# A gated linear attention feeding a SiLU layer: weights to float32 by bits, products read from PSUM, the reverse scan first, and a range check that reads its data late

## The chip, the cores and the metric

The kernel runs on one core of a Trainium2 chip. The core has five engines with a queue each: PE (TensorE, matrix products), DVE (VectorE), ACT (ScalarE), POOL (GpSimd) and SP (SyncE, which here only issues DMAs). Each works off its queue in order and waits on semaphores for the others. The metric is the device time of one execution in microseconds (us). The kernel before takes 747.67 us (median of 3 runs, 747.03 to 749.17).

## The reference

```python
# q, k, v, alpha: float32 (4, 8, 768, 48); moe_w_in (384, 2048), moe_w_out (2048, 384): float64
state = zeros(B, H, D, D)
for t in range(S):
    state = alpha[:, :, t, :, None] * state + einsum('bhd,bhe->bhde', k[:, :, t], v[:, :, t])
    y[:, :, t] = einsum('bhd,bhde->bhe', q[:, :, t], state)
x = y.transpose(0, 2, 1, 3).reshape(B * S, H * D)          # (3072, 384)
h = x @ w_in
out = (h * (1.0 / (1.0 + exp(-h))) @ w_out).astype(float32)
```

`alpha` lies between 0.8 and 1. Both weight matrices arrive as float64 (two 32-bit words an element, 512 KB for a piece of 128 by 512).

## The kernel before

**Chunks.** The sequence is cut into 6 chunks of 128 tokens for each of 4 batches: 24 chunks, numbered n, four batches after each other for one stretch of the sequence. A chunk passes through four stages. `products`: PE transposes a, k and q of the chunk (L484), ACT copies them out of PSUM (L486, L489), DVE builds the running product `p` of alpha forward (a scan, L493), its end (`least`, L497) and the end's reciprocal (`inv`, L498), and backward products `r` by a second scan (L499) that starts from `inv`; POOL multiplies q by `p` (L501) and DVE k by `r` (L502). `scores`: PE forms k·q for 8 heads (L513), DVE masks them (`g`, L517), PE transposes the scaled k back (L521) and ACT copies it (L523). `values`: PE multiplies the scores by v (L530), adds q times the carried state (L535), ACT copies the result (`x`, L539); PE then forms the chunk's addition to the state (L543), DVE adds it (L548) and POOL multiplies the state by the chunk's decay (L550). `bridge`: PE transposes the result into the layout of the next layer (L560), ACT copies it (`xt`, L561).

**The layer.** `moe` takes one stretch (4 chunks, 512 tokens): 16 pieces of 3 products each (L570) with a SiLU behind each on ACT (L573), then 4 outputs of 16 products each (L579), copied by ACT (L584) and stored (L586). That is 32 pieces a stretch, 192 in all; they are the filler that PE works on between chunk stages.

**Weights.** A piece of float64 is loaded by SP (L453), and turned into float32 by nine instructions: four on DVE (L456, L459, L461, L464), three on POOL (L457, L458, L465), one on ACT (L463). There are 12 pieces of `w_in` and 16 of `w_out`.

**Order.** A loop over 27 steps emits stage `products` of chunk `step`, `scores` of the chunk before it, `values` of the one before that, `bridge` of the one before that; behind each stage it emits weight pieces (steps 0 to 7: `w_in`) or layer pieces up to a share that grows evenly. A layer piece is held back until its four chunks have passed `bridge`. A scheduler behind the language then fixes each engine's queue; it may move an instruction past others of the program. PSUM tiles: `ps_t` (2 buffers), `ps_g`, `ps_y`, `ps_s` (1 each), `ps_m` (2).

**Check.** The largest |alpha| of every chunk (`most`, L477) and the smallest decay are kept; at the end they give a flag. If it is 0, a second, general function runs everything again.

## Time and profile before

| | |
|---|---|
| median of 3 runs | 747.67 us |
| the profiled execution's own time | 747.51 us |
| its span, first to last instruction | 745.8 us |
| PE busy | 690.5 us (93%) |
| DVE, ACT, POOL busy | 226.5, 157.5, 126.4 us |
| mean granted clock of PE | 0.941 |
| moved by DMA | 36.74 MB |

The page gives the busy share of each engine in 40 slices of the span (18.6 us each), and the clock granted to PE in the same slices. PE counts as busy while matmuls are in flight, at whatever clock; so a busy PE at clock 0.5 does half the work. In the lists of the profile a matmul of float32 stands as two records (a transpose as one); "x96" in the chain counts records. A time behind "<-" is idle time that ended when the named engine delivered.

### The profile page before, as it was taken

How to read it: one execution, taken by the hardware profiler on the slowest of the kernel's cores; microseconds unless marked ns; L12 is line 12 of the kernel's file. 1: busy time of each engine (PE TensorE's matmuls, PEld its weight loads, DVE VectorE, ACT ScalarE, POOL GpSimd, SP SyncE). 2: the span in 40 equal slices, each digit the busy share in tenths (PEclk: the TensorE clock that was granted, in tenths of full speed). 3: DMA queues.
4: the chain of work that ended last, by engine and by line, in shares of the span. 5: the costliest groups of instructions: out<-in, count | busy, mean ns of one | idle time of the engine just before them, and what ended most of it. 6: DMA issues, size and time to landing. Idle time of an engine off the chain costs nothing.

```text
span 745.8 us, 7166 instructions
## 1 busy us (share of the span) xinstructions
PE 690.5 (93%) x2874; PEld 428.9 (58%) x2874; DVE 226.5 (30%) x353; ACT 157.5 (21%) x290; POOL 126.4 (17%) x155
## 2 busy tenths in 40 slices
PE   4657779997899999999999999999999999999996
PEld 2656755554565556674556684456674456754553
DVE  4898695447422121212213142002171001000000
ACT  2322223322212221122211122211132210122100
POOL 4467364335311010100101010001010000000000
PEclk9755598998999999999999989999999999999999
DMA  9767377315220102031010221011010000000000
GB/s 155 150 140 158 91 133 136 88 53 137 64 53 22 33 11 43 22 68 28 11 32 25 50 54 22 0 22 32 19 26 1 0 11 11 22 2 1 0 21 25
DMA packets 107371, 36.74 MB, mean 49 GB/s; under 512 B 100672, under 2 KB 103744, under 8 KB 107328
## 3 DMA queue, kind: packets, MB, share of 16 engines
q1 hardware_dynamic: 107328, 36.19, 23.6%
q8 instruction: 25, 0.41, 0.2%
q14 instruction: 18, 0.15, 0.1%
HBM read 31.46 MB, written 4.72 MB: 49 GB/s over the span
## 4 chain that ended last, share of the span: by engine, by line
PE 82%; DVE 10%; POOL 2%; issue 1%; ACT 1%; DMA 1%; SPq 1%; ACTq 0%; POOLq 0%; DVEq 0%
PE ps_m L570 33%; PE ps_m L579 30%; PE ps_y L530 5%; PE ps_g L513 4%; PE ps_t L484 3%; PE ps_y L535 2%; PE ps_s L543 2%; DVE r L499 2%; DVE p L493 2%; PE ps_t L521 1%; DVE g L461 1%; DVE g L464 1%; DVE g L459 1%; POOL st L550 1%; DVE g L456 1%
## 5 line engine op out<-in xcount | busy, mean ns | idle before, releaser
L579 PE MATMUL ps_m<-w_out,g 128*128 128x384 f32 x768 | 257.8, 490 | 6.6 <-POOL w_out L465 6.6
L570 PE MATMUL ps_m<-xt,w_in 128*128 128x512 f32 x576 | 254.4, 597 | 1.3 <-ACT g L573 0.8
L579 PEld LDWEIGHTS ps_m<-w_out,g 128*128 128x128 f32 x768 | 143.3, 191 | 101.6 <-POOL w_out L465 9.5
L570 PEld LDWEIGHTS ps_m<-xt,w_in 128*128 128x128 f32 x576 | 108.4, 192 | 128.0 <-issue 125.9
L573 ACT ACTIVATE g<-ps_m 128x512 f32<-128x512 f32 x96 | 57.2, 597 | 192.2 <-PE ps_m L570 192.2
L550 POOL TENSOR_TENSOR st<-st,p 128x384 f32<-128x384 f32 x20 | 19.1, 955 | 316.9 <-DVE st L548 258.4
L517 DVE TENSOR_TENSOR g<-ps_g,mask 128x512 f32<-128x512 f32 x48 | 31.1, 684 | 135.2 <-PE ps_g L513 135.0
L513 PE MATMUL ps_g<-qt,kt 48*128 48x128 f32 x384 | 36.8, 330 | 27.3 <-DVE kt L502 26.5
L530 PEld LDWEIGHTS ps_y<-vn,g 128*128 128x128 f32 x384 | 51.7, 209 | 11.0 <-issue 7.1
L530 PE MATMUL ps_y<-vn,g 128*128 128x48 f32 x384 | 51.6, 286 | 5.1 <-issue 4.1
L513 PEld LDWEIGHTS ps_g<-qt,kt 48*128 48x128 f32 x384 | 30.7, 226 | 39.8 <-issue 19.9
L501 POOL TENSOR_TENSOR qt<-qt,p 128x512 f32<-128x512 f32 x24 | 29.9, 1246 | 125.5 <-ACT qt L489 91.9
L548 DVE TENSOR_TENSOR st<-ps_s,st 48x192 f32<-48x192 f32 x40 | 14.2, 355 | 102.5 <-PE ps_s L543 102.0
L477 DVE TENSOR_REDUCE most<-an 128x1 f32<-128x512 f32 x24 | 16.2, 679 | 79.0 <-DMA an<-in_alpha_dram 79.0
L499 DVE TENSOR_TENSOR_SCAN r<-al,inv 128x516 f32<-128x516 f32 x24 | 39.3, 1639 | 0.6
L584 ACT COPY o<-ps_m 128x384 f32<-128x384 f32 x24 | 11.5, 479 | 129.9 <-PE ps_m L579 114.8
L493 DVE TENSOR_TENSOR_SCAN p<-al,one 128x516 f32<-128x516 f32 x24 | 30.5, 1270 | 18.6 <-POOL st L550 15.3
L502 DVE TENSOR_TENSOR kt<-kt,r 128x512 f32<-128x512 f32 x24 | 17.7, 737 | 59.5 <-ACT kt L489 57.7
L489 ACT COPY qt<-ps_t 128x512 f32<-128x512 f32 x24 | 14.0, 585 | 61.7 <-PE ps_y L535 56.4
L463 ACT ACTIVATE g<-g 128x384 f32<-128x384 int32 (+1 forms) x28 | 16.0, 570 | 51.0 <-DVE g L461 40.2
L464 DVE SCALAR_TENSOR_TENSOR g<-bits,g 128x384 f32<-128x384 uint32 (+1 forms) x28 | 19.6, 699 | 22.2 <-ACT g L463 22.1
L484 PE MATMUL ps_t<-ident,an 128*128 128x128 f32 x96 | 18.8, 330 | 7.9 <-DMA an<-in_alpha_dram 4.8
(56 smaller groups left out, 430.5 us busy)
## 6 DMA issues: line engine op xcount, KB each, us to landing
bits<-in_moe_w_in_dram SPq DMA_DIRECT2D x12, 512.0 KB, 3.8
bits<-in_moe_w_out_dram SPq DMA_DIRECT2D x16, 384.0 KB, 3.3
an<-in_alpha_dram SPq DMA_DIRECT2D x24, 192.0 KB, 4.1
kn<-in_k_dram SPq DMA_DIRECT2D x24, 192.0 KB, 4.0
qn<-in_q_dram SPq DMA_DIRECT2D x24, 192.0 KB, 4.3
vn<-in_v_dram SPq DMA_DIRECT2D x24, 192.0 KB, 2.9
out_dram<-o SPq DMA_DIRECT2D x24, 192.0 KB, 1.9
```

Source lines behind the costliest of these rows:

```text
L464: dve.scalar_tensor_tensor(m, lo, 2.0**-52, m, ALU.mult, ALU.add)
L484: pe.transpose(ps[:, j, :], c[name][:, 2 * j : 2 * j + 2, :], ident)
L493: dve.tensor_tensor_scan(p[:, 0 : n_all - 1], sg[:, 0 : n_all - 1], one[:, 0 : n_all - 1], 0.0, ALU.mult, ALU.add)
L499: dve.tensor_tensor_scan(r[:, n_all - 2 :: -1], sg[:, n_all - 1 : 0 : -1], iv[:, n_all - 2 :: -1], 0.0, ALU.mult, ALU.add)
L501: gps.tensor_tensor(out["q"], out["q"], tokens(p), ALU.mult)
L513: pe.matmul(ps[:, u, j, :], lhsT=c["kp"][r, j, :], rhs=c["qp"][r, j, :], start=True, stop=True)
L517: dve.tensor_tensor(g[:, u], ps[:, u], mask[:, None, :].to_broadcast([128, NP, C]), ALU.mult)
L530: pe.matmul(py[:, h, :], lhsT=g[:, h % 2, h // 2, :], rhs=vn[:, h, :], start=(h == 0), stop=(ci == 0 and h == H - 1), skip_group_check=True)
L550: gps.tensor_tensor(s, s, c["pc"][:, :, None].to_broadcast([128, NP, 2 * D]), ALU.mult)
L570: pe.matmul(ps, lhsT=w_in[:, t, f * 128 : (f + 1) * 128], rhs=xt[:, t, :], start=(t == 0), stop=(t == NKT - 1))
L573: act.activation(gf, ps, AF.Silu)
L579: pe.matmul(ps, lhsT=gs[f][:, b * C : (b + 1) * C], rhs=w_out[:, f, :], start=(f == 0), stop=(f == NFT - 1))
```

## The change

- **Weights by bits.** A piece takes five instructions and none on POOL: ACT scales the low words into `up`; DVE shifts and masks the high words into the weight tile, ors in the two top bits, and adds `up` as integers. The built program shows that addition as one instruction of its own kind over 16-bit halves (1024 to a row of 512 words).
- **Products.** `u`, the backward products, come first, from a scan that starts from ones; the forward scan `p` then starts from the reciprocal of the chunk's decay (`all`). DVE multiplies k and q straight from PSUM, so two ACT copies and a POOL product a chunk are gone. `ps_t` has 3 buffers in place of 2, and `ps_s` is gone: the state's addition uses `ps_y` too.
- **State.** A function of its own, `states`, emitted behind `bridge`; the decay is multiplied in ahead of it, in `scores`, on DVE.
- **Check.** `most` is gone. `audit` reads alpha again (9 pieces of 512 KB) and both weight matrices again (28 pieces), each reduced by DVE: the largest of alpha, largest and smallest exponent word of the weights. Up to two audit pieces are emitted a step from step 10 on.
- **Schedule.** 5 slots a step; `w_in` in steps 1 to 6, the layer from step 7 (before: 0 to 7, from 8); `w_out` two pieces ahead of each layer piece. `raw`, the buffers of the loads, 4 in place of 2.
- The memsets on POOL ahead of the first scan are in another order.

```diff
-    raw = pool("raw", 2)
+    raw = pool("raw", 4)
-    gpool = pool("gpool", NFT + 4)
+    gpool = pool("gpool", NFT + 3)
-    ps_t = pool("ps_t", 2, PS)
+    ps_t = pool("ps_t", 3, PS)
-    ps_s = pool("ps_s", 1, PS)
...
-    for t in seg + inv:
-        gps.memset(t, 0.0)
+    gps.memset(seg[0], 0.0)
     gps.memset(one, 0.0)
     gps.memset(one[:, 0 : NP * W + 1 : W], 1.0)
+    for t in inv + seg[1:]:
+        gps.memset(t, 0.0)
...
-            e = gpool.tile([128, 512], I32, name="g")[:, 0:n]
-            dve.tensor_scalar(e, hi, 20, 0x7FF, ALU.logical_shift_right, ALU.bitwise_and)
-            gps.tensor_scalar(e, e, 1151, 896, ALU.min, ALU.max)
-            gps.tensor_scalar(e, e, -896.0, float(1 << 23), ALU.add, ALU.mult)
-            dve.scalar_tensor_tensor(e, hi, -(1 << 31), e, ALU.bitwise_and, ALU.bitwise_or)
...
-            gps.tensor_tensor(dst, m, e.bitcast(F32), ALU.mult)
+            up = gpool.tile([128, 512], I32, name="g")[:, 0:n]
+            act.activation(up, lo, AF.Copy, scale=2.0**-29)
+            w = dst.bitcast(I32)
+            dve.tensor_scalar(w, hi, 3, 0x3FFFFFFF, ALU.logical_shift_left, ALU.bitwise_and)
+            dve.scalar_tensor_tensor(w, hi, -(1 << 30), w, ALU.bitwise_and, ALU.bitwise_or)
+            dve.tensor_tensor(w, w, up, ALU.add)
             yield
...
+    def audit():
+        flat = alpha.rearrange("b h s d -> (b h s d)").rearrange("(p c) -> p c", p=128)
+        todo = [(flat[:, c : c + AW], AW, 0) for c in range(0, flat.shape[1], AW)]
+        if wide:
+            todo += [(moe_w_in[t * 128 : t * 128 + 128, c : c + 512], 512, 1)
+                     for c in range(0, DF, 512) for t in range(NKT)]
+            todo += [(moe_w_out[f * 128 : f * 128 + 128, :], HD, 1) for f in range(NFT)]
...
+        for src, n, kind in todo:
+            t = raw.tile([128, 512, 2], I32, name="bits")
...
+            for which, op in ((0, ALU.max), (1, ALU.min)):
+                if kind == 1 or which == 0:
+                    dve.tensor_reduce(seen[kind][which][:, i : i + 1], x, axis=AX, op=op,
+                                      apply_absolute_value=True)
+            yield
...
+        u = work.tile([128, end + 1], F32, name="u")
+        dve.tensor_tensor_scan(u[:, end - 1 :: -1], sg[:, end:0:-1], one[:, end:0:-1],
                                0.0, ALU.mult, ALU.add)
...
-        gps.tensor_tensor(out["q"], out["q"], tokens(p), ALU.mult)
-        dve.tensor_tensor(out["k"], out["k"], tokens(r), ALU.mult)
+        dve.tensor_tensor(kp, ps["k"], tokens(u), ALU.mult)
...
+        dve.tensor_tensor_scan(p[:, 0:end], sg[:, 0:end], iv[:, 0:end], 0.0, ALU.mult, ALU.add)
+        dve.tensor_tensor(qp, ps["q"], tokens(p), ALU.mult)
...
+        if ci > 0:
+            s = st[b].rearrange("p j u e -> p j (u e)")
+            dve.tensor_tensor(s, s, c["all"][:, :, None].to_broadcast([128, NP, 2 * D]), ALU.mult)
...
+    def states(n):
...
+            ps = ps_y.tile([128, NP, 2, D], F32, name="ps_y")
...
+    def fill(step, slot):
+        nonlocal done
+        if step < FIRST:
+            if step >= 1:
+                convert(0, ((step - 1) * SLOTS + slot + 1) * n_conv[0] // ((FIRST - 1) * SLOTS))
+            return
+        if step > FIRST + 2 and slot in (0, 2):
+            next(audits, None)
+        share = total * ((step - FIRST) * SLOTS + slot + 1) // (SLOTS * (STEPS - FIRST))
+        while done < share and done // PIECES * B + B <= bridged:
+            convert(1, 2 * done + 2)
+            next(filler)
+            done += 1
```

The instructions change place in the queues. Three places matter below.

DVE, in the start, chunk 7 before (p to kt: L493 to L502; L456 to L464 belong to weight pieces):

```order
L493 SCALAR_TENSOR_TENSOR p<-al_141,one 128x516
L517 TENSOR_TENSOR g<-ps_g,mask 128x512
L497 TENSOR_SCALAR least<-p 128x4
L517 TENSOR_TENSOR g<-ps_g,mask 128x512
L498 RECIPROCAL inv_143<-least 128x4
L459 SCALAR_TENSOR_TENSOR g<-bits,g 128x512
L499 SCALAR_TENSOR_TENSOR r<-al_141,inv_143 128x516
L461 TENSOR_SCALAR g<-bits 128x512
L502 TENSOR_TENSOR kt<-kt,r 128x512
```

DVE, the same start, now: from the forward scan of chunk 5 to the backward scan of chunk 6 (L522 `u`, L530 `p`, L532 `qp`, L588 the state out of `ps_y`, L464 to L466 two weight pieces):

```order
L530 SCALAR_TENSOR_TENSOR p<-al_138,inv_140 128x516
L464 TENSOR_SCALAR w_in<-bits 128x512
L532 TENSOR_TENSOR qp<-ps_t,p 128x512
L465 SCALAR_TENSOR_TENSOR w_in<-bits,w_in 128x512
L464 TENSOR_SCALAR w_in<-bits 128x512
L466 ISA w_in<-w_in,g 128x1024
L465 SCALAR_TENSOR_TENSOR w_in<-bits,w_in 128x512
L588 COPY st_154<-ps_y 48x4x48
L466 ISA w_in<-w_in,g 128x1024
L588 COPY st_154<-ps_y 48x4x48
L522 SCALAR_TENSOR_TENSOR u<-al_137,one 128x516
```

The state leaves `ps_y` behind six instructions of two weight pieces, and the next chunk's scan stands behind it.

PE, in the start, now: from the scores of chunk 5 to the state of chunk 4 (L543 scores, L551 k back, L598 bridge, L563 and L568 values, L517 the next chunk's a, L608 the layer, L580 the state):

```order
L543 MATMUL ps_g<-qp,kp 128x128 x8
L551 MATMUL ps_t<-ident,kp 128x128 x4
L598 MATMUL ps_t<-ident,x 128x128 x3
L563 MATMUL ps_y<-vn,g 128x48 x8
L568 MATMUL ps_y<-st_151,qp 128x96 x4
L517 MATMUL ps_t<-ident,an_101 128x128 x4
L608 MATMUL ps_m<-xt,w_in 128x512
L580 MATMUL ps_y<-vn,kn 128x96 x4
```

Values (L563) need `ps_y` free, so they wait for the second L588 above; the next chunk's a stands behind them.

DVE, later, now: chunk 9, with the audit's reductions (L499) between its own instructions:

```order
L522 SCALAR_TENSOR_TENSOR u<-al_138,one 128x516
L499 TENSOR_REDUCE seen_1225<-bits 128x1
L525 TENSOR_TENSOR kp<-ps_t,u 128x512
L527 TENSOR_SCALAR least<-u 128x4
L556 TENSOR_TENSOR st_152<-st_152,u 128x384
L528 RECIPROCAL inv_140<-least 128x4
L499 TENSOR_REDUCE seen_1226<-bits 128x1
L530 SCALAR_TENSOR_TENSOR p<-al_138,inv_140 128x516
L499 TENSOR_REDUCE seen_1225<-bits 128x1
L499 TENSOR_REDUCE seen_1226<-bits 128x1
L547 TENSOR_TENSOR g<-ps_g,mask 128x512 x2
```

In the kernel before, a chunk at this place has one reduction of its own (L477) and the last pieces of `w_out`; now the queue of DVE carries all 65 reductions of the audit between the scan of chunk 8 and that of chunk 11, and each waits for its load.

133 lines of the change are left out of this document (67 added, 66 removed).

## The prediction

> **What bounds the kernel now.** First the page: busy shares, the slices, and the chain of waits by engine.
>
> ```profile
> PE 690.5 (93%) x2874; PEld 428.9 (58%) x2874; DVE 226.5 (30%) x353; ACT 157.5 (21%) x290; POOL 126.4 (17%) x155
> PE   4657779997899999999999999999999999999996
> DVE  4898695447422121212213142002171001000000
> PEclk9755598998999999999999989999999999999999
> PE 82%; DVE 10%; POOL 2%; issue 1%; ACT 1%; DMA 1%; SPq 1%; ACTq 0%; POOLq 0%; DVEq 0%
> ```
>
> PE sets the end from slice 7 on (130 us) and is not full before; there DVE is the busy one and PE's clock is low. The list of the chain (start, us, what, records) gives PE's price for each kind of work at full clock, and two marks of the start.
>
> ```profile
> 33.41 1.14 DVE p L493
> 104.90 1.23 DVE p L493
> 114.96 9.56 PE ps_m L570 x18
> 519.41 0.87 PE ps_t L484 x8
> 525.88 1.09 PE ps_g L513 x16
> 535.30 1.72 PE ps_y L530 x16
> 537.02 0.93 PE ps_y L535 x8
> 537.95 0.91 PE ps_s L543 x8
> 657.31 41.47 PE ps_m L570 x96
> 698.78 41.29 PE ps_m L579 x128
> ```
>
> The whole of PE's work at these prices: the layer 6 x (41.47 + 41.29) = 496.6; scores 24 x 1.09 = 26.2; values 24 x 1.72 = 41.3 and 20 x 0.93 = 18.6; states 20 x 0.91 = 18.2; 440 transposes (12 a chunk for a, k, q, 3 for the bridge, 4 for k back in 20 chunks) x 0.109 = 47.9. Sum 648.7 us. The span is 745.8, so 97 us are lost: 5.7 behind the last product (698.78 + 41.29 = 740.1); and the rest on two sides of 114.96, where the first long run of the layer begins. Ahead of it the queue holds 8 chunks' transposes and scores, 6 values, 6 states, 4 bridges and 6 layer products: 46.7 us of work, so 68.3 are lost. Behind it 602.0 of work take 625.1: 23.1 lost. Where, the table by windows says (us, PE busy, PEld, DVE, ACT, POOL; clock, DMA share, GB/s):
>
> ```profile
> 12.50:15.00 2.50, 0.00 (x0) 0.00 (x0) 1.41 (x4) 0.56 (x1) 0.00 (x0) 1.00 1.49 164
> 20.00:25.00 5.00, 5.00 (x41) 4.49 (x40) 3.12 (x7) 2.39 (x5) 0.00 (x0) 0.74 1.17 289
> 40.00:100.00 60.00, 46.37 (x256) 42.02 (x256) 48.50 (x71) 17.74 (x33) 35.09 (x33) 0.58 0.59 129
> 114.96:160.00 45.04, 45.04 (x173) 24.91 (x173) 19.82 (x38) 14.40 (x28) 14.92 (x21) 0.96 0.44 92
> 160.00:200.00 40.00, 33.43 (x117) 19.27 (x116) 27.94 (x46) 9.11 (x18) 21.70 (x30) 0.91 0.37 104
> 437.00:448.00 11.00, 9.16 (x69) 8.80 (x69) 6.83 (x10) 3.11 (x6) 2.79 (x3) 0.75 0.48 81
> 543.00:561.00 18.00, 16.42 (x135) 13.99 (x134) 13.21 (x19) 6.49 (x13) 3.33 (x4) 1.00 0.09 23
> 645.00:657.00 12.00, 11.32 (x87) 9.05 (x85) 1.39 (x3) 2.90 (x7) 0.00 (x0) 1.00 0.05 18
> ```
>
> From 160 to 200 the layer waits for pieces of `w_out`: 6.6 idle and 33.4 x (1 - 0.91) = 3.0 of slow clock, 9.6 together. The others (idle plus slow clock): 1.8, 4.1, 1.6, 0.7; 5.3 are scattered. From 40 to 100 DVE is busy 81% and PE 77% at clock 0.58: each waits for the other.
>
> **The change, part by part.**
>
> *The start.* Chunk 2's scan starts at 33.41, chunk 7's at 104.90: 14.3 us a step, of which DVE works 0.81 x 14.3 = 11.6 and waits 2.7. What a step costs DVE now comes from these rows (groups: count, busy, mean ns; then single instructions: start, us; then shortest/median/longest ns):
>
> ```profile
> L477 DVE TENSOR_REDUCE most<-an 128x1 f32<-128x512 f32 x24 | 16.2, 679 | 79.0 <-DMA an<-in_alpha_dram 79.0
> L517 DVE TENSOR_TENSOR g<-ps_g,mask 128x512 f32<-128x512 f32 x48 | 31.1, 684 | 135.2 <-PE ps_g L513 135.0
> L548 DVE TENSOR_TENSOR st<-ps_s,st 48x192 f32<-48x192 f32 x40 | 14.2, 355 | 102.5 <-PE ps_s L543 102.0
> L497 DVE TENSOR_SCALAR least<-p 128x4 f32<-128x4 f32 x24 | 8.8, 366 | 0.6
> L498 DVE RECIPROCAL inv<-least 128x4 f32<-128x4 f32 x24 | 4.3, 177 | 0.6
> 9.54 1.22 DVE L493 TENSOR_TENSOR_SCAN p<-al,one 128x516 f32<-128x516 f32 x1
> 110.00 0.40 DVE L461 TENSOR_SCALAR g<-bits 128x512 int32<-128x512 int32 x1
> 111.19 0.68 DVE L464 SCALAR_TENSOR_TENSOR g<-bits,g 128x512 f32<-128x512 uint32 x1
> L461 DVE TENSOR_SCALAR g<-bits x28: 346/538/1494, 25.9 to 192.8; 128x384 int32<-128x384 int32 x16, 128x512 int32<-128x512 int32 x12
> L499 DVE TENSOR_TENSOR_SCAN r<-al,inv x24: 1215/1951/1965, 14.5 to 561.9; 128x516 f32<-128x516 f32 x24
> L502 DVE TENSOR_TENSOR kt<-kt,r x24: 665/692/1180, 16.8 to 621.1; 128x512 f32<-128x512 f32 x24
> L501 POOL TENSOR_TENSOR qt<-qt,p 128x512 f32<-128x512 f32 x24 | 29.9, 1246 | 125.5 <-ACT qt L489 91.9
> L417 POOL MEMSET al<- 128x517 f32 x2 | 1.1, 532 | 0.0
> ```
>
> The same instruction takes 0.40 or 1.49 (L461), a scan 1.22 or 1.95: the long ones run beside POOL (L501 and its like). The change takes all such work from POOL, so I use the short ones. Two scans 2 x 1.22, two products 2 x 0.69, the small pair 0.54, scores 2 x 0.68, state 2 x 0.36 make 6.4; two weight pieces, each 0.40 + 0.68 + the integer addition. No row shows that addition. Its bounds: 0.68, the row of 512 words with two inputs, and twice that, 1.36, if it takes its 1024 halves one by one; I take 0.68, the nearest by bytes. So 2 x 1.76 = 3.5 and 10.0 a step (11.3 at the other bound). The products from PSUM are priced as g (0.684, which reads PSUM), no dearer than kt from SBUF (0.692).
>
> [...]
>
> Waits remain: values cannot enter `ps_y` before the second copy of the last state, which now stands behind two weight pieces, and the next a and its scan are queued behind values. PE's part of a step is 6.7 us at full clock and twice that at 0.5. So a step lies between 10.0 (DVE never waits) and 12.7 (it waits as before); I take 11.5. It starts sooner, too: the scan of chunk 0, 9.54 before, has three memsets of 0.53 fewer ahead of it on POOL: 8. Up to the scan of chunk 3, DVE's queue holds three chunks' scans, products and small pairs (3 x 4.4), two pairs of scores, three pieces, one state: 22; with 3 us of waits for PE, chunk 3 at 33 (where chunk 2 was). Chunk 7: 33 + 4 x 11.5 = 79; the layer's run as far behind as before (10.1): 89.1.
>
> Loads stay hidden: 8 chunks of 0.786 MB at 164 GB/s (the slice with chunk loads alone) and 12 pieces of 0.524 MB at 289 are 38 + 22 = 60 us of 79. Their waits would show if the mean of 129 GB/s were a limit (98 us), but the DMA share there was 0.59.
>
> *`w_out`.* The stall of 9.6 goes, since pieces come two ahead of each layer piece. DVE then needs 2 x (0.35 + 0.54 + 0.54) = 2.9 for a layer piece of 41.47 / 16 = 2.6, eight times: 2.4 late; 6.3 with the dear addition. I take 4. (0.54 is the shortest of this row.)
>
> ```profile
> L464 DVE SCALAR_TENSOR_TENSOR g<-bits,g x28: 544/679/1668, 29.7 to 194.6; 128x384 f32<-128x384 uint32 x16, 128x512 f32<-128x512 uint32 x12
> bits<-in_moe_w_in_dram SPq DMA_DIRECT2D x12, 512.0 KB, 3.8
> ```
>
> *The late check.* 17.3 MB at 289 GB/s are 60 us of loads; 9 x 1.36 + 24 x 0.68 + 32 x 0.51 = 45 of DVE (two times and three quarters of 0.68 for 1024 and 384 words), against 16.2 saved (L477). They lie in three steps, each 9.6 layer pieces and a chunk: 9.6 x 2.6 + 6.7 = 31.5, so 95 us of PE. DVE's own work there is 3 x 7 = 21; 66 of 95, hidden. Without cover it is 45 on the path.
>
> *Stretches with nothing to fill.* The share grows evenly while the layer waits for four bridges; the queue now has one chunk more without layer products beside it. The windows from 437 to 657 lost 6.4 over some five such chunks; one more and a few waits behind reductions: 2.5.
>
> *Sum.* Start 89.1. PE's work left then: the queue has 3.0 more done there (chunk 8's transposes and 3 layer products, less part of the scores), 648.7 - 49.7 = 599.0. Losses 23.1 - 9.6 + 4 + 2.5 = 20.0. End 5.7. Span 713.8; the profiled run was 1.7 above its span (747.51), 0.16 below the median: **715 us**.
>
> **Rivals.**
>
> *Cold start.* The step stays 14.3, since PE at half clock and `ps_y` rule it. For it: PE stood at 0.50 while it was busy all the time (us, PE busy, clock, DMA share, GB/s).
>
> ```profile
> 87.50:90.00 2.50, 2.50 (x13) 0.50 0.01 2
> 95.00:97.50 2.50, 2.50 (x25) 1.00 0.24 45
> ```
>
> Then 33 + 57 + 10 = 100, and 726 us. *Warm start.* PE works nearly without pause and is granted 1.00 as at 95; steps of 10.0, the run at 83, no loss at `w_out`: 715 - 6 - 4 = 705. [...]
>
> *The check blocks DVE (slower).* Its reductions stand in the queue of DVE between the scans of chunks 8 and 11. If each of 37 pieces came only after the one before was reduced, it would cost 3.8 + 2 x 0.68 = 5.2, or 192 us, 213 with the chunks' own 21: 118 more than PE's 95, 833 us. It decides above (95 + 32 - 21) / 37 = 2.9 us a piece. Against it: 4 buffers, and 289 GB/s is 1.8 us a piece.
>
> *It doesn't do what it says.* The flag comes out 0 and the general function runs: the layer alone is 497 again, 1212 us or more. A negative weight's high word, taken as an absolute value, mirrors the exponent range (898 to 1150 about 1024), so it should hold.
>
> **The numbers.** Forecast (708 to 722) 0.56, cold 0.22, warm 0.13, blocked 0.06 (a third of it near 2.9 us, no change), flag 0.03. Faster by over 0.3% (what a measurement can tell): 0.91; within: 0.02; slower: 0.07. The range takes in warm with a little more (701) and cold with the dear addition, 8 us (734).
>
> **What would show it.** Right: DVE's scans 10 to 12.5 us apart from chunk 3 to 7, the first long run of the layer near 89, no idle PE behind `w_out`, scans of 1.22 throughout, PE busy about 660. Wrong: the integer addition above 1.4 us; idle DVE in front of L588 or L522 of over 4 us a step; DVE idle on the audit's loads while PE waits for k or q; anything of the general function.

## The result, and the profile after

The changed kernel takes 692.31 us (median of 4 runs, 691.06 to 698.05) where the kernel before took 747.61 beside it. The ratio on record, which is not quite the quotient of these medians (0.9260), is 0.9272, 95% interval 0.9219 to 0.9326. The forecast was 715 us with a range from 701 to 734, so the time lies below the range. The profiled execution took 691.06 us, its span is 689.3.

| | before | after | forecast |
|---|---|---|---|
| scan of chunk 3 starts | 41.10 us | 29.00 | 33 |
| from there to the scan of chunk 7 (4 steps) | 63.8 | 37.49 | 46 |
| first long run of the layer | 114.96 | 78.86 | 89.1 |
| from there to PE's end | 625.1 | 605.0 | 619.0 |
| behind PE's end | 5.7 | 5.4 | 5.7 |
| span | 745.8 | 689.3 | 713.8 |

First the page of the changed kernel: busy time of engines, three rows of slices (17.2 us each), and the chain by engine.

```profile
PE 668.8 (97%) x2874; PEld 410.9 (60%) x2874; DVE 227.3 (33%) x414; ACT 132.6 (19%) x242; POOL 6.2 (1%) x27
PE   6889999999999999999999999999999999999996
DVE  4999986878130221303020600213440001000000
PEclk9979999999999999999999999999999999999999
PE 85%; DMA 2%; DVE 1%; ACT 1%; issue 0%; ACTq 0%; SPq 0%
```

PE is nearly full from slice 3 on (before: from slice 7, with a stall in slices 9 and 10) and its clock is low in one slice only (0.7). DVE had 10% of the chain and has 1%. It is as busy in total as it was (227.3, before 226.5), but nearly without a gap from 20 to 100 us (76.5 of 80), and POOL has only the memsets and constants at the start.

Next, the changed kernel's queue of DVE (start, us, line): the reverse scans of chunks 0, 2, 3, 5, 6 and 7, and two instructions of the step of chunk 5.

```profile
7.28 1.23 DVE L522 TENSOR_TENSOR_SCAN u<-al,one 128x516 f32<-128x516 f32 x1 [5.94 <-ACT al L519]
...
18.33 1.23 DVE L522 TENSOR_TENSOR_SCAN u<-al,one 128x516 f32<-128x516 f32 x1
...
29.00 1.23 DVE L522 TENSOR_TENSOR_SCAN u<-al,one 128x516 f32<-128x516 f32 x1
...
48.04 1.23 DVE L522 TENSOR_TENSOR_SCAN u<-al,one 128x516 f32<-128x516 f32 x1
...
53.17 0.68 DVE L532 TENSOR_TENSOR qp<-ps_t,p 128x512 f32<-128x512 f32 x1
53.77 0.68 DVE L465 SCALAR_TENSOR_TENSOR w_in<-bits,w_in 128x512 int32<-128x512 int32 x1
...
57.26 1.23 DVE L522 TENSOR_TENSOR_SCAN u<-al,one 128x516 f32<-128x516 f32 x1
...
66.49 1.22 DVE L522 TENSOR_TENSOR_SCAN u<-al,one 128x516 f32<-128x516 f32 x1
```

From 48.04 to 57.26 DVE runs 17 instructions whose durations add up to 10.28 us, in 9.22 us: 14 of them start 0.07 to 0.09 us before the recorded end of the one ahead (53.17 + 0.68 is 53.85, and the next starts at 53.77), the other three just behind it; the mean is 0.06. DVE does not wait in this step.

PE's queue at the start of the layer:

```profile
78.86 15.91 PE L608 MATMUL ps_m<-xt,w_in 128*128 128x512 f32 x36
```

The table by windows (us, PE busy, PEld, DVE, ACT, POOL; clock, DMA share, GB/s), first of the kernel before:

```profile
0.00:100.00 100.00, 66.57 (x392) 59.08 (x392) 74.22 (x110) 29.05 (x52) 54.37 (x71) 0.68 0.75 141
100.00:220.00 120.00, 108.30 (x444) 64.69 (x444) 66.81 (x114) 31.64 (x59) 47.62 (x61) 0.94 0.39 89
220.00:660.00 440.00, 435.59 (x1824) 263.87 (x1823) 85.46 (x130) 85.35 (x159) 24.44 (x24) 0.99 0.12 25
```

and of the changed one, with the window of its slow clock:

```profile
0.00:100.00 100.00, 86.15 (x512) 62.96 (x513) 87.62 (x172) 37.54 (x67) 6.18 (x27) 0.95 1.02 215
100.00:220.00 120.00, 119.98 (x485) 70.71 (x484) 62.89 (x109) 21.80 (x40) 0.00 (x0) 1.00 0.63 180
220.00:660.00 440.00, 438.84 (x1807) 263.54 (x1806) 76.79 (x134) 71.78 (x132) 0.00 (x0) 1.00 0.12 23
35.00:46.00 11.00, 10.71 (x61) 9.63 (x61) 9.48 (x18) 3.25 (x6) 0.00 (x0) 0.57 0.99 204
```

With idle time and slow clock (busy time x (1 - clock)) added, PE lost 33.4 + 21.3 = 54.7 us in the first 100 us before and 13.9 + 4.3 = 18.2 now; 11.7 + 6.5 = 18.2 from 100 to 220 before and nothing now; 4.4 of idle time and a few of slow clock from 220 to 660 before, and 1.2 now.

The groups of DVE between 8 and 100 us, in the changed kernel (count, busy, mean ns):

```profile
L522 DVE TENSOR_TENSOR_SCAN u<-al,one 128x516 f32<-128x516 f32 x9 | 11.1, 1229 | 7.1 <-ACT al L519 7.0
L466 DVE CUSTOM_DVE_ANT_0 w_in<-w_in,g 128x1024 uint16<-128x1024 uint16 x12 | 8.2, 681 | 1.5 <-ACT g L462 1.4
L465 DVE SCALAR_TENSOR_TENSOR w_in<-bits,w_in 128x512 int32<-128x512 int32 x12 | 8.1, 676 | 0.0
L525 DVE TENSOR_TENSOR kp<-ps_t,u 128x512 f32<-128x512 f32 x9 | 6.2, 686 | 0.3
L464 DVE TENSOR_SCALAR w_in<-bits 128x512 int32<-128x512 int32 x12 | 5.0, 414 | 0.0
```

The integer addition takes 0.68 us (the lower of its two bounds), the scans 1.23 throughout, and the product from PSUM 0.69.

### The profile page after: what moved, and what is told of

Same layout as the page of the kernel before. It is cut to its first block, busy times and chain, and to the rows that moved or that the text cites. A ratio compares the mean times of both kernels' runs of the same rounds, so it can differ in the third digit from the quotient of the medians.

```text
span 689.3 us, 7061 instructions
## 1 busy us (share of the span) xinstructions
PE 668.8 (97%) x2874; PEld 410.9 (60%) x2874; DVE 227.3 (33%) x414; ACT 132.6 (19%) x242; POOL 6.2 (1%) x27
## 4 chain that ended last, share of the span: by engine, by line
PE 85%; DMA 2%; DVE 1%; ACT 1%; issue 0%; ACTq 0%; SPq 0%
PE ps_m L617 36%; PE ps_m L608 33%; PE ps_y L563 5%; PE ps_t L517 3%; PE ps_g L543 3%; PE ps_y L568 2%; PE ps_y L580 2%; DMA bits<-in_moe_w_out_dram 2%; PE ps_t L551 1%; PE ps_t L598 1%; DVE w_out L466 0%; DVE w_out L465 0%; ACT x L572 0%; DVE u L522 0%; ACT g L611 0%
## 5 line engine op out<-in xcount | busy, mean ns | idle before, releaser
L608 PE MATMUL ps_m<-xt,w_in 128*128 128x512 f32 x576 | 251.7, 594 | 1.6 <-ACT g L611 1.1
L608 PEld LDWEIGHTS ps_m<-xt,w_in 128*128 128x128 f32 x576 | 107.6, 190 | 129.7 <-issue 126.2
L611 ACT ACTIVATE g<-ps_m 128x512 f32<-128x512 f32 x96 | 57.2, 596 | 180.2 <-PE ps_m L608 180.2
L586 DVE TENSOR_TENSOR st<-ps_y,st 48x192 f32<-48x192 f32 x32 | 11.3, 354 | 144.2 <-PE ps_y L580 143.9
L563 PEld LDWEIGHTS ps_y<-vn,g 128*128 128x128 f32 x384 | 47.6, 198 | 5.7 <-issue 1.9
L563 PE MATMUL ps_y<-vn,g 128*128 128x48 f32 x384 | 47.8, 278 | 0.6 <-DVE st L588 0.3
L522 DVE TENSOR_TENSOR_SCAN u<-al,one 128x516 f32<-128x516 f32 x24 | 29.5, 1230 | 52.4 <-ACT al L519 52.0
L499 DVE TENSOR_REDUCE seen<-bits 128x1 f32<-128x384 int32 (+2 forms) x65 | 42.2, 687 | 12.7 <-DMA bits<-in_moe_w_out_dram 5.4
L622 ACT COPY o<-ps_m 128x384 f32<-128x384 f32 x24 | 11.5, 479 | 153.5 <-PE ps_m L617 121.3
L525 DVE TENSOR_TENSOR kp<-ps_t,u 128x512 f32<-128x512 f32 x24 | 16.6, 690 | 63.4 <-PE ps_t L517 61.4
L532 DVE TENSOR_TENSOR qp<-ps_t,p 128x512 f32<-128x512 f32 x24 | 16.5, 686 | 59.3 <-PE ps_y L568 59.2
L543 PEld LDWEIGHTS ps_g<-qp,kp 48*128 48x128 f32 x384 | 24.5, 195 | 13.4 <-issue 8.8
L543 PE MATMUL ps_g<-qp,kp 48*128 48x128 f32 x384 | 29.4, 294 | 2.9 <-DVE qp L532 2.9
L530 DVE TENSOR_TENSOR_SCAN p<-al,inv 128x516 f32<-128x516 f32 x24 | 29.5, 1229 | 0.5
L572 ACT COPY x<-ps_y 128x384 f32<-128x384 f32 x24 | 11.5, 479 | 79.5 <-PE ps_y L568 73.3
L580 PEld LDWEIGHTS ps_y<-vn,kn 128*128 128x128 f32 x160 | 21.4, 198 | 7.2 <-ACT x L572 3.4
L553 ACT COPY kn<-ps_t 128x512 f32<-128x512 f32 x20 | 11.7, 587 | 62.0 <-PE ps_t L551 62.0
L517 PE MATMUL ps_t<-ident,an 128*128 128x128 f32 x96 | 17.9, 300 | 5.9 <-POOL one L420 4.1
L580 PE MATMUL ps_y<-vn,kn 128*128 128x96 f32 x160 | 23.0, 285 | 0.5 <-ACT x L572 0.2
```

The costliest lines, as they stand in the source:

```text
L499: dve.tensor_reduce(seen[kind][which][:, i : i + 1], x, axis=AX, op=op, apply_absolute_value=True)
L517: pe.transpose(ps[name][:, j, :], c[name][:, 2 * j : 2 * j + 2, :], ident)
L522: dve.tensor_tensor_scan(u[:, end - 1 :: -1], sg[:, end:0:-1], one[:, end:0:-1], 0.0, ALU.mult, ALU.add)
L525: dve.tensor_tensor(kp, ps["k"], tokens(u), ALU.mult)
L530: dve.tensor_tensor_scan(p[:, 0:end], sg[:, 0:end], iv[:, 0:end], 0.0, ALU.mult, ALU.add)
L543: pe.matmul(ps[:, u, j, :], lhsT=c["kp"][r, j, :], rhs=c["qp"][r, j, :], start=True, stop=True)
```

## The experiments

Each run stands against the kernel before on the same chip. The ratios on record are compared with 0.9272 of the changed kernel; 0.01 is 7.5 us.

| run | median us | ratio | 95% interval |
|---|---|---|---|
| conversion by bits alone, on the kernel before | 715.94 | 0.9583 | 0.9553 to 0.9613 |
| changed, former conversion | 727.65 | 0.9734 | 0.9704 to 0.9764 |
| changed, POOL products beside | 742.39 | 0.9928 | 0.9907 to 0.9949 |
| changed, POOL memsets beside | 694.68 | 0.9316 | 0.9270 to 0.9362 |
| changed, products from SBUF | 701.98 | 0.9392 | 0.9362 to 0.9421 |
| changed, check of alpha in the start | 705.94 | 0.9441 | 0.9404 to 0.9478 |
| before, without the check of alpha | 740.30 | 0.9895 | 0.9860 to 0.9929 |
| conversion by bits, without the check | 708.08 | 0.9455 | 0.9418 to 0.9491 |
| changed, no second reading | 694.22 | 0.9283 | 0.9254 to 0.9312 |
| changed, former order of steps | 689.89 | 0.9216 | 0.9183 to 0.9249 |
| changed, forward scan first | 697.11 | 0.9325 | 0.9281 to 0.9369 |
| changed, two buffers for raw words | 696.11 | 0.9299 | 0.9256 to 0.9341 |
| changed, own tile for the states | 698.97 | 0.9324 | 0.9269 to 0.9380 |
| changed, one more product on DVE a piece | 698.54 | 0.9353 | 0.9314 to 0.9393 |
| changed, six pieces of `w_in` later | 688.17 | 0.9217 | 0.9172 to 0.9262 |
| ... and spread evenly | 684.55 | 0.9152 | 0.9116 to 0.9189 |
| ... nine pieces later | 681.04 | 0.9103 | 0.9071 to 0.9135 |

### What POOL costs

**The conversion alone.** The conversion by bits is put into the kernel before; all else stays.

```diff
-            (the nine instructions, three of them on POOL)
+            up = gpool.tile([128, 512], I32, name="g")[:, 0:n]
+            act.activation(up, lo, AF.Copy, scale=2.0**-29)
+            w = dst.bitcast(I32)
+            dve.tensor_scalar(w, hi, 3, 0x3FFFFFFF, ALU.logical_shift_left, ALU.bitwise_and)
+            dve.scalar_tensor_tensor(w, hi, -(1 << 30), w, ALU.bitwise_and, ALU.bitwise_or)
+            dve.tensor_tensor(w, w, up, ALU.add)
```

> The kernel before with only the conversion of the weights by bits put in (three VectorE instructions and one of ScalarE a piece, none of POOL); order of steps, places of the pieces, check, products and loads as before. Theory A (most of the gain is POOL's work taken from beside VectorE): chunk 2 to chunk 7 take 11.5 to 12.5 us a step in place of 14.3 and the stall behind the start shrinks, 725 to 735. Theory B (the order of the steps, the check moved out of the start and the earlier weights are most of it): 740 to 747. Theory C (conversion alone makes all of it): 700 or less.

Measured 715.94: 31.5 us of the 55 come from the conversion, more than theory A gave it and less than all. Chunk 2's scan starts at 30.41 and chunk 7's at 86.01, 11.1 us a step. The table by windows of this run:

```profile
0.00:100.00 100.00, 73.50 (x469) 60.07 (x470) 76.43 (x125) 36.51 (x65) 23.96 (x41) 0.83 0.85 161
100.00:220.00 120.00, 117.82 (x483) 69.09 (x482) 46.55 (x81) 30.75 (x59) 8.12 (x8) 1.00 0.37 80
220.00:660.00 440.00, 435.94 (x1785) 259.61 (x1784) 78.48 (x120) 86.47 (x160) 22.44 (x22) 1.00 0.11 23
```

Of the 18.2 us lost from 100 to 220 before, 2.2 are left here, with the former order of steps and the former places of `w_out`. The stall of `w_out` was a price of the conversion, not of the places.

**The former conversion in the changed kernel.**

> The changed kernel with the former nine-instruction conversion of the weights (four of them on VectorE, three on POOL) put back, all else as changed. Theory A (the start is set by VectorE's queue, and POOL beside it stretches VectorE's instructions): a piece costs 0.40 us more of VectorE work, and a share of 17 instructions a step is stretched as in the kernel before (a scan 1.22 to 1.95, a first pass 0.40 to 0.54 and more), 2 to 4 us a step over six steps: the layer's first long run comes at 90 to 103 and the time is 704 to 717, with the scans of the start near 1.9 us. Theory B (no stretching that matters, only the work counts): 12 x 0.40 = 5 us, 697. Theory C (the new order of the steps is the gain and the conversion is covered): 692 to 694.

Measured 727.65, 35 us more: past the end of theory A (the edit is the one above, turned round). Chunk 2's scan starts at 18.42 and chunk 7's at 80.32, 12.4 us a step, with scans of up to 2.02. That is the theory's mechanism. On top of it PE idled 9.5 us between 100 and 140 us and had a clock of 0.87 there (changed kernel 1.00), since `w_out` was late again; the theory had left that out.

**POOL beside, with nothing waiting for it.** The two runs above also change what DVE waits for. So three products on scratch tiles were put on POOL beside each piece.

```diff
...
+            for _ in range(3):
+                gps.tensor_tensor(scr[0][:, 0:n], scr[0][:, 0:n], scr[1][:, 0:n], ALU.mult)
```

> The changed kernel with three POOL products of 128x512 (128x384 for w_out) on scratch tiles beside each weight piece; nobody waits for them, so that only their being beside VectorE's work can cost anything. Theory A (instructions of VectorE with both operands in SBUF are stretched beside POOL: scans 1.23 to 1.95, the first pass of a piece 0.40 to 0.8, while products from PSUM stay at 0.69): 2 to 4 us a step over six steps and as much again for w_out, 704 to 722, scans of up to 1.95 in the trace. Theory B (only dependences on POOL cost): 692 to 694 and scans of 1.23.

Measured 742.39: 50 of the 55 us are gone, though no instruction waits for POOL. (POOL is busier here, 94.7 of the first 100 us, than it was before the change, 54.4, so this is more than what it cost there.) The groups between 8 and 100 us, of DVE and of POOL:

```profile
L468 DVE SCALAR_TENSOR_TENSOR w_in<-bits,w_in 128x512 int32<-128x512 int32 x11 | 15.2, 1384 | 0.0
L469 DVE CUSTOM_DVE_ANT_0 w_in<-w_in,g 128x1024 uint16<-128x1024 uint16 x11 | 14.5, 1319 | 0.1
L467 DVE TENSOR_SCALAR w_in<-bits 128x512 int32<-128x512 int32 x11 | 13.8, 1257 | 0.0
L527 DVE TENSOR_TENSOR_SCAN u<-al,one 128x516 f32<-128x516 f32 x7 | 12.1, 1724 | 6.8 <-ACT al L524 6.7
L530 DVE TENSOR_TENSOR kp<-ps_t,u 128x512 f32<-128x512 f32 x7 | 4.8, 687 | 0.3
L471 POOL TENSOR_TENSOR scr<-scr,scr 128x512 f32<-128x512 f32 x36 | 57.8, 1605 | 2.8
```

The three instructions of a piece go from 0.68, 0.68 and 0.41 to 1.38, 1.32 and 1.26, the scan from 1.23 to 1.72; the product that reads PSUM stays at 0.69. For the 12 pieces of `w_in` and the 14 scans of these steps that is 12 x 2.2 + 14 x 0.5 = 33 us of VectorE's time, ahead of the layer; the pieces of `w_out` come on top.

**POOL that only writes.** Eight memsets in place of the three products, to tell "POOL works" from "POOL reads SBUF".

```diff
-            for _ in range(3):
-                gps.tensor_tensor(scr[0][:, 0:n], scr[0][:, 0:n], scr[1][:, 0:n], ALU.mult)
+            for _ in range(8):
+                gps.memset(scr[0][:, 0:n], 0.0)
```

> The changed kernel with eight POOL memsets of a scratch tile of 128x512 (128x384 for w_out) beside each weight piece, some 4 us as the three products were; they write SBUF and read nothing, and nobody waits for them. Theory A (VectorE is held up where both of its operands come from SBUF and POOL reads SBUF): scans stay at 1.23, the second pass and the addition at 0.68, and if the first pass (0.41) is stretched as well it costs at most 12 x 2 x 0.5 us: 692 to 704. Theory B (any instruction of POOL beside VectorE holds it up): scans of up to 2 us again, 720 to 745.

Measured 694.68, theory A. The same groups, of this run:

```profile
L527 DVE TENSOR_TENSOR_SCAN u<-al,one 128x516 f32<-128x516 f32 x9 | 11.1, 1229 | 7.1 <-POOL scr L443 6.0 <-ACT al L524 1.0
L468 DVE SCALAR_TENSOR_TENSOR w_in<-bits,w_in 128x512 int32<-128x512 int32 x12 | 8.1, 674 | 0.0
L467 DVE TENSOR_SCALAR w_in<-bits 128x512 int32<-128x512 int32 x12 | 7.8, 646 | 0.0
L532 DVE TENSOR_SCALAR least<-u 128x4 f32<-128x4 f32 x9 | 2.5, 279 | 0.0
L471 POOL MEMSET scr<- 128x512 f32 x96 | 51.9, 541 | 5.5
```

POOL is busy 89.9 of the first 100 us, and the instructions with two operands in SBUF keep their times; only the first pass and the small `least`, both `TENSOR_SCALAR` with one operand there, are stretched, from 0.41 to 0.65 and from 0.16 to 0.28. (The 6.0 of waits in the scan's row lies ahead of chunk 0, whose scan starts at 7.33, in the changed kernel at 7.28.) The second pass, the addition and the scan, 1.38, 1.32 and 1.72 beside POOL's products, stand at 0.67, 0.68 and 1.23 beside its memsets, and the first pass and `least` at 0.65 and 0.28 where they took 1.26 and 0.71.

**Products from SBUF.** ACT copies k and q out of PSUM again, DVE multiplies k from there and POOL q.

```diff
-        dve.tensor_tensor(kp, ps["k"], tokens(u), ALU.mult)
+        act.copy(kp, ps["k"])
+        dve.tensor_tensor(kp, kp, tokens(u), ALU.mult)
-        dve.tensor_tensor(qp, ps["q"], tokens(p), ALU.mult)
+        act.copy(qp, ps["q"])
+        gps.tensor_tensor(qp, qp, tokens(p), ALU.mult)
```

> The changed kernel with k and q first copied from PSUM by ScalarE, k's product then read from SBUF on VectorE and q's product on POOL, as before the change. Theory A (POOL's instruction of 1.25 us stretches what VectorE does beside it by up to 0.7 us, and the copy of 0.7 us lies ahead of k's product): up to 1.4 us a step over six to eight steps, 698 to 704. Theory B (reading PSUM is the dearer way, and VectorE is rid of the q product, 0.69 us a chunk): the start is shorter, 686 to 690. Theory C (TensorE's waits set the step): 692 within 2.

Measured 701.98, 9 us more (theory A). Two of its groups, over the whole of the profiled run, which is the longest of the five (709.72; the others 701.60 to 702.50):

```profile
L526 DVE TENSOR_TENSOR kp<-kp,u 128x512 f32<-128x512 f32 x24 | 16.7, 697 | 20.2 <-ACT kp L525 18.8
...
L534 POOL TENSOR_TENSOR qp<-qp,p 128x512 f32<-128x512 f32 x24 | 33.2, 1384 | 564.3 <-ACT qp L533 499.9 <-DVE p L531 57.1 <-DVE least L528 7.3
```

The product of k takes 0.697 from SBUF and 0.69 from PSUM, so the price was right: PSUM is not dearer. DVE has 0.69 a chunk less to do here and the time is longer all the same; whether by the copies ahead of the product or by POOL beside it, this run doesn't tell. Its trace shows only where: in the first 100 us DVE is busy 71.6 (changed kernel 87.6) and PE's mean clock is 0.74 (changed kernel 0.95).

### What the check of alpha costs

**Put back into the start.** One reduction a chunk ahead of its scans, no late reading of alpha.

```diff
+        dve.tensor_reduce(most[:, n : n + 1], c["a"], axis=mybir.AxisListType.XY, op=ALU.max,
+                          apply_absolute_value=True)
         sg, iv = seg[n % NR], inv[n % NR]
...
```

> The changed kernel with the range check of alpha put back to where it was: one VectorE reduction of a chunk's a at the head of its scans, 0.68 us each, in place of the nine late reductions of alpha (the weights' check stays late). Theory A (VectorE sets the start): eight of them lie ahead of the layer's first long run, at 0.62 start to start 5 us: 696 to 699. Theory B (they lie in waits): 692 to 694.

Measured 705.94, 13 us more: neither theory. DVE's queue in this run:

```profile
8.88 0.69 DVE L513 TENSOR_REDUCE most<-an 128x1 f32<-128x512 f32 x1 [3.97 <-DMA an<-in_alpha_dram]
9.49 1.22 DVE L525 TENSOR_TENSOR_SCAN u<-al,one 128x516 f32<-128x516 f32 x1
...
22.64 1.23 DVE L525 TENSOR_TENSOR_SCAN u<-al,one 128x516 f32<-128x516 f32 x1
```

The reduction of chunk 1 stands ahead of chunk 0's scan, and waits for chunk 1's load. So the scan of chunk 0 starts at 9.49 in place of 7.28, that of chunk 2 at 22.64 in place of 18.33. So far 4.3 us are lost, with waits of 3.97 and 2.77 for loads ahead of two reductions; by chunk 7's scan (75.41 in place of 66.49) it is 8.9, with the later reductions, 0.6 each, in the queue. Over the first 100 us PE is idle 19.1 in place of 13.9 and loses 11.3 in place of 4.3 to its slow clock (busy 80.95 at 0.86), so about half of the loss is slow clock. The kernel before had the same:

```profile
8.93 0.69 DVE L477 TENSOR_REDUCE most<-an 128x1 f32<-128x512 f32 x1 [4.04 <-DMA an<-in_alpha_dram]
9.54 1.22 DVE L493 TENSOR_TENSOR_SCAN p<-al,one 128x516 f32<-128x516 f32 x1
```

**Taken out of the kernel before,** alone and with the conversion by bits.

```diff
-        dve.tensor_reduce(most[:, n : n + 1], c["a"], axis=mybir.AxisListType.XY, op=ALU.max,
-                          apply_absolute_value=True)
...
```

> The kernel before without its 24 reductions of a (the range check of alpha is left out, the flag comes from the smallest totals). Theory A (the reduction of the next chunk stands at the head of VectorE's queue and waits for that chunk's load, 4.0 and 2.8 us of idle VectorE at 8.93 and 13.52; taken away, the first scans come 2 to 4 us sooner, and the later ones save 0.6 a step): 736 to 742. Theory B (with POOL's work in the steps the reductions are covered): 745 to 748.

> The kernel before with the conversion by bits alone and without the 24 reductions of a (the range check of alpha is left out). Theory A (conversion and check together are most of the gain, as check_in_start gave 13.6 when put back): 701 to 706. Theory B (the order of the steps and the products from PSUM are needed for it): 710 to 715.

Measured 740.30, within theory A, and 708.08, between the two theories. In the first, chunk 0's scan comes at 7.39, with the memsets on POOL in their former order:

```profile
7.39 1.23 DVE L491 TENSOR_TENSOR_SCAN p<-al,one 128x516 f32<-128x516 f32 x1 [5.83 <-ACT al L484]
```

The check is worth 1.1% beside the former conversion and 1.3% beside the new one (0.9583 to 0.9455).

**The late second reading.** The changed kernel without `audit`.

```diff
-    filler, audits = ffn(), audit()
+    filler, audits = ffn(), iter(())
...
```

> The changed kernel without the second reading of weights and alpha and without its reductions; the flag comes from the smallest total alone, so the range check of weights and alpha is left out. Theory (the second reading is hidden): its 42 us of VectorE and 17.3 MB of loads lie in steps where TensorE has layer work, so the time stays the changed kernel's 692.3 within 2 us. Rival (it costs something where TensorE has nothing to fill with, or through the shared DMA engines): 684 to 689.

Measured 694.22 (0.9283, the changed kernel 0.9272): its 17.3 MB and 42 us of DVE cost nothing that shows.

### What the rest costs

**The order of the steps.** The changed kernel with the loop of the kernel before (states behind values, four places a step, `w_in` in steps 0 to 7, `w_out` one piece a place).

```diff
-    FIRST = B + 3
-    SLOTS = 5
+    FIRST = 2 * B
+    SLOTS = 4
...
-            convert(1, 2 * done + 2)
+            if done >= NFT:
+                convert(1, n_conv[1])
```

> The changed kernel with the order of the steps before the change: states right behind values, four places to fill a step, w_in over the first eight steps from step 0, the layer from step 8, w_out one piece a place and the rest at once before it is used; conversion, check, products and scans as changed. Theory A (the order of the steps is small beside conversion, check and products, and gives the few us of losses behind the start, 6.2 with the former order in the run with the conversion alone and 1.2 with the new one): 693 to 699. Theory B (the order is what takes the losses away): 702 to 712.

Measured 689.89, below both theories: the new order of steps gains nothing. Nor does it take away the losses behind the start. From 220 to 660 us, this run, and then the run with the conversion by bits and no check:

```profile
220.00:660.00 440.00, 438.92 (x1758) 259.66 (x1757) 71.07 (x124) 70.98 (x131) 0.00 (x0) 1.00 0.11 22
```

```profile
220.00:660.00 440.00, 435.94 (x1773) 259.85 (x1771) 72.89 (x110) 85.73 (x159) 22.42 (x22) 1.00 0.10 22
```

PE idles 1.1 us here and 4.1 there. Both have the former order; what lies between them is the products from PSUM, the states' decay on DVE in place of POOL, the order of the scans, the third buffer of `ps_t` with the shared `ps_y`, four buffers of `raw`, the order of the memsets, and the late check.

**Scans, buffers, tile.** Three smaller parts were undone one by one. In the first, the states' decay stays where the changed kernel has it, and with the forward scan first that no longer gives the reference's values; the work is the same in kind and number.

```diff
-        dve.tensor_tensor_scan(u[:, end - 1 :: -1], sg[:, end:0:-1], one[:, end:0:-1], ...)
...
-        dve.tensor_tensor_scan(p[:, 0:end], sg[:, 0:end], iv[:, 0:end], 0.0, ALU.mult, ALU.add)
+        dve.tensor_tensor_scan(p[:, 0:end], sg[:, 0:end], one[:, 0:end], 0.0, ALU.mult, ALU.add)
...
+        dve.tensor_tensor_scan(u[:, end - 1 :: -1], sg[:, end:0:-1], iv[:, end - 1 :: -1], ...)
```

> The changed kernel with the forward scan first and the reverse scan second, as before the change, and with q transposed ahead of k; the products still read PSUM and the number of instructions is the same. Theory A (VectorE's queue sets the start, and its work is the same): 692 within 3. Theory B (with the reverse scan first k's product is ready a scan and a product earlier, 2 us, and TensorE has k's transposes to do while VectorE does the rest): TensorE idles more in each step and its clock falls, 695 to 702.

```diff
-    raw = pool("raw", 4)
+    raw = pool("raw", 2)
```

> The changed kernel with two buffers in place of four for the raw words of the weights. Theory A (a piece's load takes 3.8 to 5 us, and with two buffers w_out's sixteen pieces, two with each piece of the layer of 2.6 us, come at two in about 6 us): the layer's SILU stands in ScalarE's queue behind a conversion that waits for its load, TensorE idles behind 75 us, 697 to 706. Theory B (loads are hidden with two buffers as well): 692 to 694.

```diff
-    ps_t = pool("ps_t", 3, PS)
+    ps_t = pool("ps_t", 2, PS)
+    ps_s = pool("ps_s", 1, PS)
...
```

> The changed kernel with the states' products in a PSUM tile of their own again and two buffers in place of three for transposes. Theory A (the third buffer is what lets the products of k and q wait in PSUM; with two the transposes of q wait for VectorE, and TensorE pauses more): 693 to 700. Theory B (sharing the tile of the values with the states is a wait that costs something): 686 to 691. Theory C (VectorE sets the start either way): 692 within 2.

Measured 697.11 (theory B), 696.11 (between the two) and 698.97 (theory A). Each median is 4 to 7 us above the changed kernel's, but each interval overlaps with its (0.9219 to 0.9326), so none of the three is shown to matter by itself. With two buffers PE idles 2.2 us from 100 to 220, where the changed kernel's idles 0.02, behind SiLUs that stand on ACT after conversions which wait for loads of `w_out` (4.78 and 3.79 us in its chain): theory A's mechanism, at a smaller price.

**One more product on DVE.** Is DVE what sets the start?

```diff
...
+            if which == 0:
+                dve.tensor_tensor(scr[0], scr[0], scr[1], ALU.mult)
```

> The changed kernel with one more VectorE product of 128x512 in SBUF behind each of the 12 pieces of w_in; nobody waits for its result. Theory A (VectorE's queue sets the start, as its slices of 9.9 busy out of 10 between 20 and 90 us say): each costs its start-to-start time of about 0.6 us, 12 x 0.6 = 7, the layer's first long run at 86 and 698 to 700 us. Theory B (TensorE's waits or its clock set the start): 692 to 694. Theory C (the longer waits also drop TensorE's clock to 0.50 in more of the start): 702 to 706.

Measured 698.54, theory A by its median (its interval just touches the changed kernel's): 12 products of 0.6 cost 6.2 us. Chunk 2's scan starts at 19.48 and chunk 7's at 72.61, 10.6 a step where the changed kernel has 9.6.

### A version that is faster than both

If DVE sets the start, pieces of `w_in` that the layer needs late should leave it. First, six of the twelve go to the first pieces of the layer:

```diff
-                convert(0, ((step - 1) * SLOTS + slot + 1) * n_conv[0] // ((FIRST - 1) * SLOTS))
+                convert(0, ((step - 1) * SLOTS + slot + 1) * 6 // ((FIRST - 1) * SLOTS))
...
-            convert(1, 2 * done + 2)
+            convert(0, 7 + done)
+            convert(1, 2 * done - 4)
```

> The changed kernel with six pieces of w_in converted in the first steps, one in each, and the other six one by one with the first pieces of the layer; w_out begins four pieces of the layer later, two a piece. Theory A (VectorE sets the start): six pieces of 1.6 us are 9.7 less ahead of the layer's first long run; TensorE's own work of 6.7 a step then gets near the bound, so that 4 to 9 of it come through: 683 to 688. Theory B (TensorE's waits or its clock set the start): 690 to 693. Theory C (the pieces are late for the layer, since VectorE is busy up to 97 us): 693 to 699, TensorE idle between 80 and 110 us.

Measured 688.17, at the edge of theory A; PE stood idle 3.7 us between 60 and 100. The chain of waits of this run, and its wait:

```profile
84.27 6.07 DMA bits<-in_moe_w_out_dram
...
90.43 0.04 ACT g L462
...
90.89 0.59 ACT g L611
```

```profile
PE ps_m L608 <- ACT g L611: 3.6, 5, 1.3
```

The layer's SiLU (L611) stands on ACT behind the conversion of a piece of `w_out` (L462) that waits for its load. So the pieces were spread:

```diff
-            convert(0, 7 + done)
-            convert(1, 2 * done - 4)
+            convert(0, 7 + done // 2)
+            convert(1, done + 1)
```

> Six pieces of w_in in the first steps as in the run with w_in later, then one piece of w_in with every second piece of the layer and one of w_out with each, in place of one and two. Theory A (in that run the layer's SILU stood on ScalarE behind conversions that waited for loads of w_out, 3.7 us of idle TensorE between 60 and 100 us): most of it goes, 683 to 686. Theory B (the pieces of w_in are now late for the layer's columns): 690 or more. Theory C (no change): 688 within 2.

Measured 684.55 (theory A). Then three pieces in the start in place of six (`* 3`, `convert(0, 4 + 3 * done // 4)`, `convert(1, done)`):

> As the run with the pieces spread over the layer, with three pieces of w_in in the first steps in place of six, the other nine over the first eleven pieces of the layer, and w_out one with each. Theory A (TensorE sets the start by now, and VectorE has too much beside the layer): 684 to 689. Theory B (VectorE still sets the start: three pieces of 1.6 us less): 680 to 683.

Measured 681.04 (theory B): DVE still set the start. The page of this run:

```profile
PE   5999999999999999999999999999999999999996
PEclk9999999999999999999999999999999999999999
```

It is 68 us faster than the kernel before that ran beside it (749.05; 0.9103) and, by intervals that don't overlap, faster than the changed one. Of the 9.8 us between the two profiled spans, 4.1 are idle time of PE in the first 100 us (13.9 to 9.7) and 4.3 its slow clock there, which is gone.

## Why the prediction was wrong

The direction and the mechanism of the start were right, and the sizes were off: 713.8 of span forecast, 689.3 measured. Two terms of the sum failed: the step between scans (11.5, it took 9.37) and the losses behind the start (20.0, of which 6.0 came). The errors are -10.2 in *the start*, -14.0 in the losses of the *sum*, -0.3 at the end: -24.5.

**The start, chunk 3's scan** (33 forecast, 29.00 measured). The first scan was put at 8 because of three memsets fewer on POOL. That cause was wrong. With the memsets as before and the reductions gone it comes at 7.39; what held it at 9.54 was the reduction of chunk 1, waiting for its load; that my 8 lay near the 7.28 measured was luck. I had read that row (L477) as 0.68 us of work and passed over the 79 us of waits in it. From the first scan on I added 22 of work and 3 of waits, 25; it took 21.7.

**The start, the step** (11.5 forecast, 9.37 measured, below my bound of 10.0). DVE hardly waited: the lower end was the case, and I took the middle. And the lower end itself was too high: durations add up to more than the time, since the recorded durations of neighbours overlap by 0.06 us in the mean, about 1 us a step. The durations were right (6.4 + 3.5 forecast; 10.28 - 0.53 = 9.75 in the step shown). One thing was missing, the states' decay on DVE (0.53 from chunk 4 on). Together 4 x 2.1 = 8.5 too much. The layer's first long run then stood 12.4 behind chunk 7's scan, not 10.1: 2.3 too little. -4.0 - 8.5 + 2.3 = -10.2.

***w_out*.** That the stall of 9.6 goes is right. That it goes because pieces come two ahead isn't: the conversion alone, with the former places, leaves 2.2 of the 18.2 lost from 100 to 220, and with the new places and the former conversion PE idles 9.5 again. The pacing loss of 4 didn't come (PE idles 0.02 us from 100 to 220). For the dear addition the working has 6.3 where its own rows give 8 x (2 x 1.97 - 2.6) = 10.7; the addition was not dear, so only the top of the range would have moved. (The last step of the sum, 713.8 + 1.7 + 0.16, is 715.7 and was written as 715.)

**The late check.** Right: hidden.

**Stretches with nothing to fill, and the rest of the losses.** I added 2.5, and carried over 13.5 (23.1 - 9.6) from the kernel before, as if they belonged to the layer. From 114.96 to PE's end its windows hold 11.0 us of idle time and some 8 of slow clock. Without the stall's 9.6 that is 9.4; the other 4 are no wait, but prices of work that were a little too low. In the changed kernel the work left behind 78.86, counted from the trace, is 599.1 at my prices, as forecast; PE is idle 1.3 there, at clock 1.00. So of the 6.0 measured in place of 20.0, 1.3 are waits and 4.7 again my prices. The 9.4 belonged to the chunks' path and not to the layer: from 100 to 220 us they went with the conversion alone, and from 220 to 660 the idle time (4.1 to 1.1) went with the group of parts named above, not with the order of steps that I charged it to. Which part of the group it was stays open: undone one at a time in the changed kernel (scans, raw buffers, tile, products, check), none gives back more than 0.8 of it.

**The rivals.** The warm start (705) came nearest, with its step of 10.0 and no loss at `w_out`, and it got a chance of 0.13; its step and its losses were still too large. The cold one did not come, though 4.3 us of slow clock are left. They lie between 37 and 47 us, where PE is busy all the time (us, PE busy, clock, DMA share, GB/s):

```profile
37.50:40.00 2.50, 2.50 (x14) 0.50 1.02 359
40.00:42.50 2.50, 2.50 (x12) 0.50 1.21 174
42.50:45.00 2.50, 2.50 (x14) 0.50 0.40 67
```

In these 7.5 us PE was busy throughout and was granted 0.50; from 47 us on the clock is 1.00. What sets it, no run here shows.

**The range.** It ended at 701 because its lower side was built from the warm case "with a little more". What was never priced is POOL's presence itself: I used the undisturbed durations, but not that the delays they caused further on (the stall, the slow clock) had the same cause. The run with POOL beside, busier than before the change and with nothing waiting for it, takes back 50 of 55 us; its clock is 0.73 in the first 100 us (changed kernel 0.95), and from 100 to 220 its PE idles 12.8 us (0.02).

What stands, by ratios: the conversion 4.2% (0.9583), the check 1.3% more (0.9455), the products from PSUM with scans, buffers and the states' decay on DVE 2.4% more (0.9216, with the former order of steps), and the new order nothing that is shown. Products from SBUF, with ACT's copies and POOL's share, cost 1.2% in the changed kernel (0.9392, intervals apart), so the products are about half of the 2.4%; how the rest divides stays open.

## What to carry to other kernels

Before a stage is costed from its engine's queue, look at what a neighbour does to the durations in it: here the conversion without POOL gave more than half of the gain (31.5 of 55 us), and products on POOL that read SBUF, more of them than before and with nothing waiting for them, took nine tenths of it away (50 us). In a queue that never waits, take a step from the starts of its instructions and not from the sum of their durations (9.22 and 10.28 us in the step shown), and count a reduction or check that needs a fresh load as a wait at the head of the queue as well as by its own time: here chunk 2's scan came 4.3 us late by the first of them. When VectorE sets a start, put what is needed late into the stretch where TensorE has work enough, evenly, so that no activation stands behind a conversion that waits for its load: here nine pieces spread so took the time from 692.31 to 681.04 us.

## What the runs showed of the hardware that was not expected

- POOL products of 128x512 from SBUF, to which nothing is tied, stretch VectorE's second pass and addition (two SBUF operands) from 0.68 to 1.38 and 1.32 and a scan from 1.23 to 1.72 in the mean, and cost 50 us; POOL memsets for the same time stretch only the `TENSOR_SCALAR` instructions (the shift-and-mask pass from 0.41 to 0.65) and cost 2 us by the medians, within the noise. Both sides pay: POOL's own product took 1.17 us at its shortest in the kernel before and 1.61 in the mean in that run.
- A product that takes one operand from PSUM was not stretched in any of these runs (0.68 to 0.69 in the mean) and was no dearer than one from SBUF (0.697).
- The integer addition of 512 words, as 1024 halves of 16 bits, takes 0.68 us, as long as a product of 512 floats (0.69).
- In a queue that does not wait, most VectorE instructions start 0.07 to 0.09 us before the one ahead of them is recorded as ended (14 of 17 in the step shown).
- The four runs of the changed kernel span 689.3, 690.0, 691.0 and 696.2 us at mean clocks of 0.992, 0.991, 0.987 and 0.978: the lower the clock, the longer the time. Where it is lost, only profiled runs show: the changed kernel has 0.95 in the first 100 us, and the run without the second reading, whose profiled execution is its longest (698.04), has 0.86 there; from 100 us on both have 1.00. The version with nine pieces later, whose clock is 0.998 to 0.999 in all runs, lies within 1.6 us (680.6 to 682.16).
